# Hashed attention and a gated feed-forward layer on one core: row transfers on ACT's queue, preparation and weight steps at other places, another order of the products with v

## The chip, the cores and the metric

The kernel runs on one core of a Trainium2 chip. The metric is the device time of one execution in microseconds (us). Engines are named as in the profile: PE (matrix products; PEld is its weight load), DVE, ACT, POOL, and SP, which here only issues DMAs. Each engine works through its own instructions strictly in program order.

## The reference, cut to what matters

Four batches of eight heads, 768 positions, head dimension 64; then a feed-forward layer on 3072 rows of width 512 with hidden width 2048. A position attends only to positions with the same six hash bits.

```python
q_bits = (np.einsum('bhsd,dk->bhsk', q, proj) > 0)          # k_bits likewise, buckets from the bits
mask = q_bucket[:, :, :, None] == k_bucket[:, :, None, :]
scores = np.where(mask, scale * np.matmul(q, k.transpose(0, 1, 3, 2)), -1e9)
attn = np.exp(scores - scores.max(-1, keepdims=True))
attn = attn / (attn.sum(-1, keepdims=True) + 1e-09)
x = np.matmul(attn, v)                                       # heads side by side: 3072 x 512
h = x @ w_in
g = np.where(h >= 1, h, np.where(h <= -1, 0.0, (h + 1) ** 2 / 4.0))
out = g @ w_out
```

## The kernel before, in words

Every float32 operand is split into a high part and a low remainder, so that one exact product is several fp32r products. The 32 heads are worked in 16 **pairs**. A head has 12 **units** (two halves of the queries times six blocks of 128 keys), so a pair has 24. I call a unit's place in its pair its **phase**, 0 to 23; phases 0 to 11 are the even head, 12 to 23 the odd one. Units are numbered g = 0 to 383, and everything is emitted by one loop over g (written by hand; the schedule is not rearranged by anything later). For unit g the loop emits, in this order:

- `s_unit(g)`: two products on PE into one of four banks `s` (L439 and L440), then two exponentials on ACT, `ph` (L448, the high part) and the full value (L453), which goes to an SBUF tile `pf` if POOL is to subtract, and stays in the bank `s` if DVE is;
- `max_red` (L378): a row maximum on DVE over the tile `smax` that was filled at the end of the unit before, if there was one;
- `lo_unit(g-1)`: the low part `pl`, one subtraction (L39), on POOL for the key blocks that a table names, else on DVE;
- `pv_unit(g-4)`: three products with v on PE (L473, L475, L477) into one of two banks `o`. `PV_ORDER` gives the order in which a half's six blocks are taken. After the sixth, ACT copies the bank out (L483, `xs`);
- at every second unit two products `smax` (L361) for the maxima of a head that comes two heads later, at the end of phases 0, 2, 4 and so on. `smax` has one buffer, so these products wait until the reduction of the one before has read it;
- the tasks of unit g: preparation of later pairs and of the weights.

Tasks that the change touches, with the phase at which they stand before, for pairs from the third on:

- *Preparation of the pair after next* (`raw` to the operand tiles `t`): POOL does four quarters, a cast (L179) and a subtraction (L39), at phases 0, 2, 7, 11. SP issues moves between partitions (L190) at 13, 13, 14 and 18, and loads the next `raw` (L174) at 14.
- *Hash bits*: PE makes them at phases 5 and 17 (L237), ACT negates a part right there (`neg`, L243), DVE compares (L248) at 6 and 18, POOL scales at 19 (L307), SP writes four rows of bits (L316) at 20.
- *Row maxima*: at phases 5 and 17 `max_put` has ACT copy a small transposed tile `te` (L421); one DMA writes its first half as row 7 of an operand tile (`t<-te`, L423), another stores its second half (`em<-te`, L425). For heads 5 to 31, 27 of them, L423 is issued by SP; for heads 3 and 4 by ACT. The second product of a unit (L440) of that head needs row 7.
- *Weight conversion*: a block of weights is loaded as 8-byte numbers (`wraw`, SP, L78), ACT rebuilds the exponent (the scaled copy `wsq<-wraw`, L82), DVE does three steps on bits (L86, L90, L94; L86 writes in the bank `o` that `xs` was just copied from), POOL makes high and low parts (L102, L39), SP stores (`put`, L108). Twelve blocks of w_in start at phase 12 of an odd head with offsets 0, 9, 10, 11, 14, 19, 21, 23; twelve further blocks start at phase 0 of an even head with offsets 0, 9, 10, 11, 14, 16 (pairs 2 to 13). So in most pairs there are two scaled copies on ACT, at phases 9 and 21.
- `cast_v` (ACT, `va`, L323) stands at phase 6.

After unit 383 the feed-forward layer follows, from about 442 us on, which the change does not touch.

Of the kernel before, what the change touches and what calls it, by code (L numbers as in the profile page):

```python
# [11 lines left out]
F32 = mybir.dt.float32  # L12
# [29 lines left out]
def streamed(t):  # L42

    return t.rearrange("p (g r w) -> p g w r", r=2, w=4)


def into(t):
    return t.rearrange("p (g w r) -> p g w r", w=4, r=2)
# [71 lines left out]
NQK, NV, NP_ = 3, 2, 7  # L120
LAG = 4
POOL_J = (0, 3)
FROM = 4 * 12
QUARTER_J = ((0, 1, 3), (0, 3), (0, 1, 3), (0, 3))
PV_ORDER = (1, 2, 0, 4, 5, 3)
NU = 2 * NJ
SHIFT = 4


def attention(ctx, tc, wst, T1, T2, qk, v, pj, cv, x_d, s_d, e_d, tasks, shared):  # L130
    nc = tc.nc
# [286 lines left out]
    def max_put(hd):  # L418
        pr, h = hd // 2, hd % 2
        te = small.tile([2 * NJ, P], F32R, name="te")  # L420
        (nc.vector.tensor_copy if hd == 0 else nc.scalar.copy)(out=te, in_=mx.pop(hd)[0:2 * NJ, 0:P])  # L421
        if pr > 0:
            (nc.sync if hd > 4 else nc.scalar).dma_start(out=T2[pr % NQK][7:8, 0, h, :].bitcast(F32),  # L423
                                                         in_=te[0:NJ, :].bitcast(F32))
        nc.sync.dma_start(out=e_d[hd // H][hd % H:hd % H + 1, :], in_=te[NJ:2 * NJ, :].bitcast(F32))  # L425

# [2 lines left out]
    def pool_lo(g):  # L429
        return g % NJ in (QUARTER_J[g // NJ % 4] if FROM <= g < (NH - 2) * NU else POOL_J)  # L430

    def s_unit(g):
        hd, hf, j = g // NU, (g % NU) // NJ, g % NJ
        pr, h = hd // 2, hd % 2
        t1, t2 = T1[pr % NQK], T2[pr % NQK]
        sl = slice(hf * HS, (hf + 1) * HS)
        ks = slice(j * P, (j + 1) * P)
        ps = ps_s.tile([P, 512], F32, name="s")
        nc.tensor.matmul(out=into(ps[:, 0:HS]), lhsT=t1[:, 1, h, ks], rhs=streamed(t1[:, 0, h, sl]), start=True, stop=False)  # L439
        nc.tensor.matmul(out=into(ps[:, 0:HS]), lhsT=t2[:, 1, h, ks], rhs=streamed(t2[:, 0, h, sl]), start=False, stop=True)  # L440
        ph, pl = PH[g % NP_], PL[g % NP_]
        if hd >= NH - 2 and j == 4:
            pf = ps[:, 0:HS]
            nc.scalar.activation(out=pf, in_=pf, func=AF.Exp, scale=SCALE)
            nc.vector.tensor_copy(out=ph[:, 0:HS], in_=pf)
            units[g] = (pf, ph, pl)
            return
        nc.scalar.activation(out=ph[:, 0:HS], in_=ps[:, 0:HS], func=AF.Exp, scale=SCALE)  # L448
        if pool_lo(g):
            pf = work.tile([P, HS], F32, name="pf", bufs=3)  # L450
        else:
            pf = ps[:, 0:HS]
        nc.scalar.activation(out=pf, in_=ps[:, 0:HS], func=AF.Exp, scale=SCALE)  # L453
        units[g] = (pf, ph, pl)
# [7 lines left out]

    def pv_unit(n, between):
        hd, hf, jj = n // NU, (n % NU) // NJ, n % NJ
        j = PV_ORDER[jj]
        pr, h = hd // 2, hd % 2
        va, vb = VA[pr % NV], VB[pr % NV]
        _, ph, pl = units.pop(n - jj + j)
        o = obank[hf]
        w = HS if hf == 0 else HS + 8  # L470
        wa = va[:, j, h:h + 2, :].rearrange("p g d -> p (g d)")
        wb = vb[:, j, h:h + 2, :].rearrange("p g d -> p (g d)")
        nc.tensor.matmul(out=into(o[:, 0:w]), lhsT=wa, rhs=streamed(ph[:, 0:w]), start=(jj == 0), stop=False)  # L473
        between(3)
        nc.tensor.matmul(out=into(o[:, 0:w]), lhsT=wb, rhs=streamed(ph[:, 0:w]), start=False, stop=False)  # L475
        between(4)
        nc.tensor.matmul(out=into(o[:, 0:HS]), lhsT=wa, rhs=streamed(pl), start=False, stop=(jj == NJ - 1))  # L477
        if jj == NJ - 1:
            if hf == 0:
                xss[hd] = work.tile([P, S + 2], F32, name="xs")  # L480
            xs = xss[hd]
            w = HS if hf == 0 else HS + 2
            nc.scalar.copy(out=xs[:, hf * HS:hf * HS + w], in_=o[:, 0:w])  # L483
            if hf == 1:
                xss.pop(hd)
                rs, sr = 64 * h, 64 * (1 - h)
                nc.sync.dma_start(out=x_d[hd // H][rs:rs + 64, pr % (H // 2), :], in_=xs[rs:rs + 64])
                nc.sync.dma_start(out=s_d[hd // H][hd % H:hd % H + 1, :], in_=xs[sr:sr + 1, 0:S])
# [31 lines left out]
    def raw0():  # L520
        return wst.tile([P, DM, 2], I32, name="wraw").rearrange("p a b -> p (a b)").bitcast(F32)[:, 0:S].rearrange(
            "p (h s) -> p h s", h=1)
# [8 lines left out]
    def at(g, fn, *a):  # L531
        tasks[g].append((fn, a))

    first = [raw0(), raw0()]
# [106 lines left out]
    at(24, half_put, 2, 1)  # L641
    for h, g in enumerate((20, 2 * NU + 1)):
        at(g, lambda h=h: nc.gpsimd.memset(T2[0][32:33, 0, h].bitcast(F32), 0.0))
    for hd in range(NH):
        pr, h = hd // 2, hd % 2
        g = hd * NU
        if 0 < hd < NH - 2:
            gc, gt = ((30, 32), (41, 43))[hd - 1] if hd < 3 else (g + NU + SHIFT - 1, g + NU + SHIFT + 1)
            at(gc, max_clamp, hd + 2, nc.gpsimd)
            at(gt, max_tr, hd + 2)  # L650
            at(gt, max_put, hd + 2)
        if h == 0 and pr + 2 < NPAIR:
            g0 = g + (13, 2)[pr] if pr < 2 else g
            for n in range(4):
                gq = g0 + (n + (pr == 1 and n == 3) if pr < 2 else (0, 2, 7, 11)[n])
                at(gq, cast_h, pr + 2, nc.gpsimd, n % 2, n // 2)
                at(gq, low_h, pr + 2, nc.gpsimd, n % 2, n // 2)
            for n in range(2):
                at(g0 + (3 + (pr == 1) if pr < 2 else 13), move, pr + 2, n)
            at(g0 + (6 if pr < 2 else 14), move, pr + 2, 2)  # L660
            if pr + 3 < NPAIR:
                at(g0 + (7 if pr < 2 else 14), load_raw, pr + 3)
            bits_at = (((20, 1), (22, 0)), ((8, 1), (11, 0)))[pr] if pr < 2 else ((5, 1), (17, 1))
            for hf, (n, bank) in enumerate(bits_at):
                at(g + n, bits_mm, pr + 2, hf, bank)
                at(g + n + 1, bits_cmp, pr + 2, hf)
            at(g + n + 1, move, pr + 2, 3)
            if pr:
                at(g + n + 2, bits_scale, pr + 2, nc.gpsimd)
            else:  # L670
                at(g + 22, bits_scale, 2, nc.scalar, 0)
                at(g + 24, bits_scale, 2, nc.scalar, 1)
            at(g + (24, 18)[pr] if pr < 2 else g + 20, bits_put, pr + 2)
        if h == 0 and pr + 1 < NPAIR:
            gv = g + LAG + (2 if pr else 16)
            at(gv, cast_v, pr + 1, nc.scalar)
            for h, n in enumerate((1, 3) if pr < 2 else (12, 14)):
                at(gv + n, split_v, pr + 1, nc.gpsimd, h)
            if pr + 2 < NPAIR:
                at(gv + ((4, 6)[pr] if pr < 2 else 16), load_v, pr + 2)  # L680
# [7 lines left out]
    for i in range(2 * NJ):  # L688
        n = 5 * 31 + 35 * i // 4
# [500 lines left out]
def lsh_attn_ffn(ctx: ExitStack, tc: tile.TileContext, qk, v, pj, cv, w_in, w_out, out):  # L1190
    nc = tc.nc
# [8 lines left out]
    T2 = [wp.tile([P, 2, 2, S], F32R, name=f"t2_{i}") for i in range(NQK)]  # L1200
# [33 lines left out]
    def at(g, fn, *a):  # L1234
        tasks[g].append((fn, a))

    def conv(g, steps, offs):
        for fn, n in zip(steps, offs):
            at(g + n, fn)
# [6 lines left out]
    def wi_steps(i, cp, stage=None):  # L1246
        return ws.steps(win_v[:, :, i * P:(i + 1) * P, :], (P, NCT, P, 2), wih[i], wil[i], cp, stage, None, wq[i], word)
# [6 lines left out]
    for i in range(NW1):  # L1254
        if i < 2:
            conv((2 * i + 3) * NU, wi_steps(i, nc.scalar), (0, 9, 10, 11, 14 - (i == 0), 17, 19, 21))
        else:
            conv((2 * i + 3) * NU, wi_steps(i, nc.gpsimd), (0, 9, 10, 11, 14, 19, 21, 23))
    g0 = (NH - 4) * NU
    late = {}  # L1260
    for n in range(NSTG):
        i = n - (NFT - NW1)
        stage = wq[NW1 + n] if i < 0 else xdp.tile([P, DM], F32, name=f"wd{n}")
        if i < 0:
            first, late[n] = wi_steps(NW1 + n, nc.gpsimd, stage)
        elif i < 2:
            first, late[n] = wo_steps(i, nc.gpsimd, stage)
        else:
            first, late[n] = wo_steps(i, nc.scalar, stage, nc.gpsimd if i < 4 else nc.vector)
        conv((4 + 2 * n) * NU, first, (0, 9, 10, 11, 14, 16))  # L1270
    for n, g in enumerate((1, 7, 13, 25, 30, 35)):
        conv(g0 + g, late[n], (0, 5, 6))

# [1 line left out]
    for b in range(B - 1):  # L1275
        g = (b + 1) * H * NU + LAG + 4
# [32 lines left out]
    for i in range(2, NFT):  # L1309
        n = i + NFT - NW1  # L1310
# [71 lines left out]
```

## Time and profile before

| what | value |
|---|---|
| median of three runs | 928.15 us (926.03 to 929.7) |
| the profiled execution | 927.39 us, span 925.6 us |
| granted PE clock | full speed throughout |
| PE busy | 904.9 us, 98% of the span |
| DVE, ACT, POOL busy | 746.3, 667.1, 352.3 us |

The profiled execution's own time is 1.8 us over its span and 0.8 us under the median. The attention part is the first 442 us. There PE, DVE and ACT are all nearly full, POOL is busy for 350 us of it, and PE's queue is in program order; what delays PE there delays the end.

### The profile page before, as it was taken

Reading aid. Unit: us, or ns where it says so; the run is one execution under the profiler, and the core shown is the slowest. Engines: PE = TensorE matmul, PEld = TensorE weight load, DVE = VectorE, ACT = ScalarE, POOL = GpSimd, SP = SyncE. Lnnn points to the kernel's source line nnn. Section 1 sums busy time; section 2 is a strip of 40 time slices with the busy share of each in tenths; the row PEclk is TensorE's granted clock in tenths of the full one; section 3 lists DMA queues with packets and bytes.
Section 4 is the critical chain, followed back from the end, with each engine's and each line's share of the span. In section 5 each row is a group of like instructions: output and inputs, shape, how many; then the busy total and the mean of one; then the engine's idle time right before and its main releaser. Section 6 shows DMA issues by size and latency. Waiting matters only on the chain.

```text
span 925.6 us, 15771 instructions
## 1 busy us (share of the span) xinstructions
PE 904.9 (98%) x5050; PEld 846.4 (91%) x5050; DVE 746.3 (81%) x1319; ACT 667.1 (72%) x1471; POOL 352.3 (38%) x464
## 2 busy tenths in 40 slices
PE   8999999999999999999999999999999999999997
PEld 7789999999998999999999998989999999999996
DVE  8988889888897889887798888878877788765564
ACT  7889998999988999999656566555565555554454
POOL 7877777888787787778100000000000000000000
PEclk9999999999999999999999999999999999999999
DMA  5774676666666676564496388987559564464431
GB/s 159 195 201 109 181 195 194 191 181 180 175 179 187 188 193 184 140 185 123 144 307 228 114 245 299 317 259 204 149 152 271 156 200 127 147 178 126 125 91 68
DMA packets 95689, 167.66 MB, mean 181 GB/s; under 512 B 14532, under 2 KB 52536, under 8 KB 95608
## 3 DMA queue, kind: packets, MB, share of 16 engines
q1 hardware_dynamic: 95344, 166.63, 62.3%
q8 instruction: 40, 0.66, 0.3%
q14 instruction: 41, 0.34, 0.1%
q10 hardware_dynamic: 264, 0.03, 0.0%
HBM read 106.13 MB, written 33.96 MB: 151 GB/s over the span
## 4 chain that ended last, share of the span: by engine, by line
PE 71%; DVE 11%; ACT 7%; DMA 5%; issue 4%; POOL 1%; DVEq 0%; ACTq 0%; SPq 0%; POOLq 0%
PE y L913 24%; PE h L1145 16%; PE h L1050 6%; DMA t<-te 4%; PE s L440 4%; PE smax L361 4%; PE o L477 3%; PE o L473 3%; PE o L475 3%; PE s L439 3%; DVE nm L378 3%; DVE pl L39 3%; PE o L237 2%; ACT ph L448 2%; ACT s L453 1%
## 5 line engine op out<-in xcount | busy, mean ns | idle before, releaser
L448 ACT ACTIVATE ph<-s 128x384 fp32r<-128x384 f32 x380 | 193.0, 508 | 31.3 <-PE s L440 28.5
L39 POOL TENSOR_TENSOR pl<-pf,ph 128x384 fp32r<-128x384 f32 x154 | 156.0, 1019 | 67.9 <-ACT pf L453 67.7
L378 DVE TENSOR_REDUCE nm<-smax 128x1 f32<-128x768 f32 x168 | 160.1, 953 | 22.5 <-PE smax L361 19.4
L39 DVE TENSOR_TENSOR pl<-s,ph 128x384 fp32r<-128x384 f32 x230 | 123.6, 549 | 22.6 <-ACT s L453 18.3
L878 DVE SCALAR_TENSOR_TENSOR t<-t 128x384 f32<-128x384 f32 x128 | 71.3, 557 | 85.9 <-ACT z L873 85.6
L440 PE MATMUL s<-t 128*128 128x384 f32 x384 | 126.2, 329 | 3.5 <-DMA t<-te 3.4
L477 PE MATMUL o<-pl,va 128*128 128x384 f32 x384 | 125.7, 327 | 1.0 <-POOL pl L39 0.6
L473 PE MATMUL o<-ph,va 128*128 128x392 f32 (+1 forms) x384 | 126.0, 328 | 0.6 <-DVE neg L248 0.6
L475 PE MATMUL o<-ph,vb 128*128 128x392 f32 (+1 forms) x384 | 125.8, 328 | 0.0
L439 PE MATMUL s<-t 128*128 128x384 f32 x384 | 125.7, 327 | 0.0
L913 PE MATMUL y<-t,ghi 128*128 128x512 f32 x384 | 118.3, 379 | 0.7 <-DMA wc<-tmp 0.7
L453 ACT ACTIVATE s<-s 128x384 f32<-128x384 f32 x226 | 115.7, 512 | 0.0
L361 PE MATMUL smax<-t 128*128 128x384 f32 x336 | 85.9, 337 | 4.0 <-DVE nm L378 3.3
L883 ACT CAST ghi<-z 128x384 fp32r<-128x384 f32 x129 | 64.9, 503 | 32.0 <-DVE z L879 31.7
L873 ACT ACTIVATE z<-t,m 128x384 f32<-128x384 f32 x128 | 78.8, 615 | 4.2
L440 PEld LDWEIGHTS s<-t 128*128 128x128 f32 x384 | 72.5, 189 | 6.3 <-DMA t<-te 6.1
L913 PEld LDWEIGHTS y<-t,ghi 128*128 128x128 f32 x384 | 71.0, 189 | 7.4 <-ACT ghi L883 1.3
L453 ACT ACTIVATE pf<-s 128x384 f32<-128x384 f32 x154 | 77.5, 503 | 0.0
L1145 PE MATMUL h<-wbig,t 128*128 128x384 f32 x399 | 76.6, 326 | 0.3 <-DVE wsq L1164 0.3
L879 DVE TENSOR_TENSOR z<-t,z 128x384 f32<-128x384 f32 x128 | 71.4, 558 | 4.5
L477 PEld LDWEIGHTS o<-pl,va 128*128 128x128 f32 x384 | 72.6, 189 | 2.4 <-POOL pl L39 1.5
L913 PE MATMUL y<-woh,glo 128*128 128x512 f32 x192 | 73.1, 381 | 0.8 <-DVE glo L887 0.8
(208 smaller groups left out, 2003.3 us busy)
## 6 DMA issues: line engine op xcount, KB each, us to landing
t<-wc SPq DMA_DIRECT2D x92, 256.0 KB
t<-t SPq DMA_DIRECT2D x60, 384.0 KB
wraw<-wc SPq DMA_DIRECT2D x76, 256.0 KB
raw<-in_qk_dram SPq DMA_DIRECT2D x14, 768.0 KB
wraw<-in_w_in_dram SPq DMA_DIRECT2D x16, 512.0 KB
wraw<-in_w_out_dram SPq DMA_DIRECT2D x16, 512.0 KB
t<-ed SPq DMA_DIRECT2D x36, 192.0 KB
xd<-xs SPq DMA_DIRECT2D x32, 192.5 KB
```

The costliest lines, as they stand in the source:

```text
L39: eng.tensor_tensor(out=out, in0=a, in1=b, op=ALU.subtract)
L361: nc.tensor.matmul(out=into(ps[:, 0:HS]), lhsT=t2[:, 0, h, i * P:(i + 1) * P], rhs=streamed(t2[:, 1, h, hf * HS:(hf + 1) * HS]), start=Tru ...
L378: nc.vector.tensor_reduce(out=nmp(hd)[:, i:i + 1], in_=smax[hd][:, :, 0:HS], axis=AX.XY, op=ALU.max, negate=True)
L439: nc.tensor.matmul(out=into(ps[:, 0:HS]), lhsT=t1[:, 1, h, ks], rhs=streamed(t1[:, 0, h, sl]), start=True, stop=False)
L440: nc.tensor.matmul(out=into(ps[:, 0:HS]), lhsT=t2[:, 1, h, ks], rhs=streamed(t2[:, 0, h, sl]), start=False, stop=True)
L448: nc.scalar.activation(out=ph[:, 0:HS], in_=ps[:, 0:HS], func=AF.Exp, scale=SCALE)
L453: nc.scalar.activation(out=pf, in_=ps[:, 0:HS], func=AF.Exp, scale=SCALE)
L473: nc.tensor.matmul(out=into(o[:, 0:w]), lhsT=wa, rhs=streamed(ph[:, 0:w]), start=(jj == 0), stop=False)
L475: nc.tensor.matmul(out=into(o[:, 0:w]), lhsT=wb, rhs=streamed(ph[:, 0:w]), start=False, stop=False)
L477: nc.tensor.matmul(out=into(o[:, 0:HS]), lhsT=wa, rhs=streamed(pl), start=False, stop=(jj == NJ - 1))
L913: nc.tensor.matmul(out=into(ys[c][m]), lhsT=g_[:, m * P:(m + 1) * P], rhs=streamed(w), start=(first and k == 0), stop=(last and k == 2))
L1145: nc.tensor.matmul(out=into(ps), lhsT=w[:, cs], rhs=streamed(x), start=(n == 0 and s not in (2, 3, 6)), stop=(n == 5), skip_group_check=True)
```

## The change

The diff, with the lines that only bear new numbers left out:

```diff
-QUARTER_J = ((0, 1, 3), (0, 3), (0, 1, 3), (0, 3))
+QUARTER_J = ((0, 2, 3), (0, 3), (0, 2, 3), (0, 3))
 PV_ORDER = (1, 2, 0, 4, 5, 3)
+PV_LATER = (1, 0, 2, 4, 3, 5)
...
         if pr > 0:
-            (nc.sync if hd > 4 else nc.scalar).dma_start(out=T2[pr % NQK][7:8, 0, h, :].bitcast(F32),
+            nc.scalar.dma_start(out=T2[pr % NQK][7:8, 0, h, :].bitcast(F32),
...
-        j = PV_ORDER[jj]
+        j = (PV_LATER if n >= FROM else PV_ORDER)[jj]
...
-                gq = g0 + (n + (pr == 1 and n == 3) if pr < 2 else (0, 2, 7, 11)[n])
+                gq = g0 + (n + (pr == 1 and n == 3) if pr < 2 else (0, 2, 6, 9)[n])
...
-                at(g0 + (7 if pr < 2 else 14), load_raw, pr + 3)
+                at(g0 + (7 if pr < 2 else 13), load_raw, pr + 3)
...
-                at(g + n + 1, bits_cmp, pr + 2, hf)
+                at(g + n + (1 if pr < 2 else 2), bits_cmp, pr + 2, hf)
...
-                at(g + n + 2, bits_scale, pr + 2, nc.gpsimd)
+                at(g + n + (2 if pr < 2 else 3), bits_scale, pr + 2, nc.gpsimd)
...
-            at(g + (24, 18)[pr] if pr < 2 else g + 20, bits_put, pr + 2)
+            at(g + (24, 18)[pr] if pr < 2 else g + 21, bits_put, pr + 2)
...
-            conv((2 * i + 3) * NU, wi_steps(i, nc.gpsimd), (0, 9, 10, 11, 14, 19, 21, 23))
+            conv((2 * i + 3) * NU, wi_steps(i, nc.gpsimd), (0, 9, 10, 11, 14, 23, 25, 24))
...
-        conv((4 + 2 * n) * NU, first, (0, 9, 10, 11, 14, 16))
+        conv((4 + 2 * n) * NU, first, (0, 9, 10, 11, 14, 16) if n < 2 else (-6, 3, 10, 11, 14, 16))
```

Two places in the program, where the later argument stands. ACT, a pair in the middle (pair 8), phases 3 to 7, before; `xs` is the copy-out of the head before, `te` the small tile of row maxima, `neg` the negated part of the bits, `va` the cast of v:

```order
L483 COPY xs<-o_142 128x386
L448 ACTIVATE ph_159<-s 128x384
L453 ACTIVATE s<-s 128x384
L448 ACTIVATE ph_160<-s 128x384
L453 ACTIVATE s<-s 128x384
L421 CAST te<-s 12x128
L243 ACTIVATE neg<-o_142 32x384
L448 ACTIVATE ph_161<-s 128x384
L453 ACTIVATE pf<-s 128x384
L323 CAST va_156<-vraw 128x6x2x64
L448 ACTIVATE ph_162<-s 128x384
L453 ACTIVATE s<-s 128x384
```

The same place on ACT in the changed kernel:

```order
L484 COPY xs<-o_142 128x386
L82 ACTIVATE wsq<-wraw 128x512
L449 ACTIVATE ph_159<-s 128x384
L454 ACTIVATE s<-s 128x384
L449 ACTIVATE ph_160<-s 128x384
L454 ACTIVATE s<-s 128x384
L422 CAST te<-s 12x128
L424 DMA t_2_83<-te 1x6x128
L244 ACTIVATE neg<-o_142 32x384
L449 ACTIVATE ph_161<-s 128x384
L454 ACTIVATE pf<-s 128x384
L324 CAST va_156<-vraw 128x6x2x64
```

The scaled copy `wsq` has come ahead of phase 4 (before, it stands after the next `xs`, at phase 9), and the issue of the row transfer has come between `te` and `neg`. At phase 17 of every pair with bits the transfer's issue comes in the same way, with no scaled copy moved there.

DVE, phases 1 to 9 of a pair, before; `nm<-smax` is the row maximum, `wsq<-wsq,wsc,o` the last weight step, `pl` the low parts:

```order
L378 TENSOR_REDUCE nm<-smax 128x1
L94 SCALAR_TENSOR_TENSOR wsq<-wsq,wsc,o_141 128x512
L378 TENSOR_REDUCE nm<-smax 128x1
L39 TENSOR_TENSOR pl_171<-s,ph_164 128x384
L378 TENSOR_REDUCE nm<-smax 128x1
L39 TENSOR_TENSOR pl_166<-s,ph_159 128x384
L39 TENSOR_TENSOR pl_167<-s,ph_160 128x384
L248 TENSOR_TENSOR neg<-o_142,neg 32x384
L378 TENSOR_REDUCE nm<-smax 128x1
L39 TENSOR_TENSOR pl_169<-s,ph_162 128x384
L378 TENSOR_REDUCE nm<-smax 128x1
```

The same place on DVE in the changed kernel:

```order
L379 TENSOR_REDUCE nm<-smax 128x1
L39 TENSOR_TENSOR pl_170<-s,ph_163 128x384
L94 SCALAR_TENSOR_TENSOR wsq<-wsq,wsc,o_141 128x512
L379 TENSOR_REDUCE nm<-smax 128x1 x2
L39 TENSOR_TENSOR pl_166<-s,ph_159 128x384
L39 TENSOR_TENSOR pl_167<-s,ph_160 128x384
L379 TENSOR_REDUCE nm<-smax 128x1
L249 TENSOR_TENSOR neg<-o_142,neg 32x384
L39 TENSOR_TENSOR pl_169<-s,ph_162 128x384
L379 TENSOR_REDUCE nm<-smax 128x1
```

The low part of phase 1 has come to DVE, ahead of the weight step, and that of phase 2 has gone to POOL; the comparison `neg` stands behind the reduction of phase 7 instead of ahead of it. The low part `pl_169` (phase 7) still stands ahead of the reduction of phase 9.

## The prediction

> **What bounds the kernel now.** I read the page first, then a table by stretches, the list of waits, and the order of time of ACT, DVE and PE over one pair.
>
> ```profile
> span 925.6 us, 15771 instructions
> PE 904.9 (98%) x5050; PEld 846.4 (91%) x5050; DVE 746.3 (81%) x1319; ACT 667.1 (72%) x1471; POOL 352.3 (38%) x464
> ...
> 60.00:420.00 360.00, 351.82 (x2094) 336.99 (x2093) 313.16 (x470) 327.24 (x801) 281.57 (x355) 1.00 0.64 178
> 442.00:925.60 483.60, 476.70 (x2541) 442.18 (x2539) 365.16 (x711) 273.19 (x516) 2.50 (x2) 1.00 0.62 186
> ```
>
> The columns of the last two rows are the stretch, its length, and busy time of PE, PEld, DVE, ACT and POOL. From 60 to 420 us, where the change acts, PE is busy for 351.8 of 360 us, but ACT for 327.2 and DVE for 313.2: ACT has only 33 us to spare over 15 pairs, about 2 us a pair. What little PE loses is in the list of waits (total, times, longest):
>
> ```profile
> PEld smax L361 <- DVE nm L378: 11.7, 27, 0.6
> PEld s L440 <- DMA t<-te: 6.1, 9, 1.2
> PE s L440 <- DMA t<-te: 3.4, 6, 0.9
> PE smax L361 <- DVE nm L378: 3.3, 14, 0.3
> ```
>
> Two waits matter: for the row transfer, 3.4 (matrix engine idle) to 6.1 us (weight load idle), and for the row maximum on DVE, 3.3 to 11.7. So at most some 18 us can be won, by nobody's being late; but much more can be lost if ACT or DVE fall behind.
>
> **The row transfers.** SP issues 27 of them; two are already issued by ACT:
>
> ```profile
> L423 SPq DMA_DIRECT2D t<-te x27: 755/765/785, 81.8 to 425.3; - x27
> L423 ACTq DMA_DIRECT2D t<-te x2: 677/704/730, 57.7 to 70.5; - x2
> ...
> 57.45 0.25 ACT L421 CAST te<-s 12x128 fp32r<-12x128 f32 x1
> 57.73 0.73 ACTq L423 DMA_DIRECT2D t<-te  x1
> 58.51 0.48 ACT L243 ACTIVATE neg<-o 32x384 f32<-32x384 f32 x1 [0.81 <-PE o L477]
> ...
> PE o L473 <- DVE neg L248: 0.6, 1, 0.6
> ```
>
> An issue is not counted as busy, but it is not free: it starts after `te` has ended, lasts 0.73 us, and ACT's next instruction starts after it. From `te` to `neg` pass 1.06 us. The last row is that very place: ACT's `neg` came late, so DVE's comparison, so PE stood still for 0.6 us. On SP the same 0.77 us costs nothing, since SP computes nothing. Twenty-seven issues are 27 x 0.7 = 19 us of ACT in all; what they cost must be followed through the queues.
>
> **The scaled copy and the transfer, phases 3 to 14.** Pair 8, ACT:
>
> ```profile
> 238.12 0.52 ACT L448 ACTIVATE ph<-s 128x384 fp32r<-128x384 f32 x1
> ...
> 239.70 0.25 ACT L421 CAST te<-s 12x128 fp32r<-12x128 f32 x1
> 240.20 0.48 ACT L243 ACTIVATE neg<-o 32x384 f32<-32x384 f32 x1 [0.25 <-PE o L237]
> ...
> 242.56 0.50 ACT L453 ACTIVATE s<-s 128x384 f32<-128x384 f32 x1
> ...
> 244.49 0.52 ACT L483 COPY xs<-o 128x384 f32<-128x384 f32 x1
> 244.85 0.73 ACT L82 ACTIVATE wsq<-wraw 128x512 f32<-128x512 f32 x1
> 245.42 0.54 ACT L448 ACTIVATE ph<-s 128x384 fp32r<-128x384 f32 x1
> ```
>
> From 238.12 on ACT runs without a gap except the 0.25 ahead of `neg`. The scaled copy takes 245.42 - 244.85 = 0.57 of ACT's time. Moved ahead of 238.12, it shifts `te` to 240.27; with an issue behind it `neg` starts 1.06 later, at 241.33 in place of 240.20. The idle 0.25 is used up, and everything on ACT from there is 1.13 late, among it the exponential of phase 7 (242.56). At phase 9 the copy is no longer there, so from 245.42 on ACT is 0.56 late. What waits for phase 7 is DVE:
>
> ```profile
> 243.16 0.56 DVE L39 TENSOR_TENSOR pl<-s,ph 128x384 fp32r<-128x384 f32 x1 [0.86 <-ACT s L453]
> 243.63 0.95 DVE L378 TENSOR_REDUCE nm<-smax 128x1 f32<-128x768 f32 x1
> 244.50 0.55 DVE L39 TENSOR_TENSOR pl<-s,ph 128x384 fp32r<-128x384 f32 x1
> 245.04 0.69 DVE L86 TENSOR_SCALAR o<-wraw 128x512 int32<-128x512 int32 x1
> 245.64 0.95 DVE L378 TENSOR_REDUCE nm<-smax 128x1 f32<-128x768 f32 x1
> 246.51 0.55 DVE L39 TENSOR_TENSOR pl<-s,ph 128x384 fp32r<-128x384 f32 x1
> 246.97 0.75 DVE L90 SCALAR_TENSOR_TENSOR o<-wsq,wsc,o 128x512 int32<-128x512 int32 x1
> 247.63 0.55 DVE L39 TENSOR_TENSOR pl<-s,ph 128x384 fp32r<-128x384 f32 x1
> 248.10 0.95 DVE L378 TENSOR_REDUCE nm<-smax 128x1 f32<-128x768 f32 x1
> ...
> 244.72 0.51 PE L361 MATMUL smax<-t 128*128 128x384 f32 x2
> 246.70 0.54 PE L361 MATMUL smax<-t 128*128 128x384 f32 x2
> 249.10 0.59 PE L361 MATMUL smax<-t 128*128 128x384 f32 x2 [0.22 <-DVE nm L378]
> ```
>
> The low part at 243.16 waited 0.86 us for ACT; from there DVE works back to back to the reduction at 248.10, and PE's products `smax` must each wait for the reduction ahead of them. The first has 0.14 of room (244.72 against 243.63 + 0.95), the last has none and already waits. In the changed kernel this run of nine instructions has the same order, so it starts 1.13 late. The reduction of phase 9 then ends at 245.71, `smax` follows 0.05 behind it (as 249.10 does behind 248.10 + 0.95), at 245.76: PE is 1.04 late, and nearly 0.1 more because two `smax` behind a wait take 0.59 in place of 0.51. The waits at phases 12 and 14 keep their size, since the whole run has moved. PE's work from there is in order and has no gap in which to make it up. Price: 1.1 us in each of pairs 4 to 13, where both edits act: **+11**. Its ends: 0 if ACT made up its lateness somewhere that the rows don't show, and 10 x 1.34 (0.57 + 0.77, nothing absorbed) = +13.4. I take 11 because each step is a row. In pairs 2 and 3 the scaled copy stays at phase 9, and the issue alone makes 1.06 - 0.50 = 0.56 each: **+1** (0 to 1.5).
>
> **The transfer's other half, phases 17 to 2.**
>
> ```profile
> 226.94 0.48 ACT L243 ACTIVATE neg<-o 32x384 f32<-32x384 f32 x1 [0.19 <-PE o L237]
> ...
> 230.36 0.49 ACT L448 ACTIVATE ph<-s 128x384 fp32r<-128x384 f32 x1 [0.20 <-PE s L440]
> ...
> 234.69 0.95 DVE L378 TENSOR_REDUCE nm<-smax 128x1 f32<-128x768 f32 x1
> ...
> 228.07 5.25 DMA t<-te
> ...
> 233.37 0.43 PE L440 MATMUL s<-t 128*128 128x384 f32 x1 [0.44 <-DMA t<-te]
> 236.10 0.49 PE L361 MATMUL smax<-t 128*128 128x384 f32 x2
> ...
> 262.66 0.59 PE L361 MATMUL smax<-t 128*128 128x384 f32 x2
> ```
>
> On SP the transfer was issued at 228.07 and landed 5.25 us later; PE waited for it at 233.37. On ACT it is issued more than a microsecond sooner and stands behind no load, so I take this wait as gone. What is late next is the reduction at 234.69, done at 235.64: without the wait PE would reach `smax` at about 235.6 in place of 236.10, and must then wait for that reduction. ACT is late here too: the idle 0.19 and 0.20 absorb 0.4 of some 0.8, so the run of DVE up to 234.69 comes 0.2 to 0.4 later. With 0.3 that `smax` stands at 236.0 and the pair wins 0.1; pair 9, which had no wait for the transfer but already one of this kind (262.66, two products in 0.59), loses 0.3. Nine pairs of the first kind and three of the second: **0**, with ends at -6.1 (the whole wait won, nothing late next) and +4.8 (12 x 0.4).
>
> The Trainium skill ("DMA: Bandwidth & Descriptors", section "Rules for kernel authors") speaks against this edit: transfers from SP, ACT and GpSimd share the same 16 DMA engines, and spreading them only saves a sequencer's issue time. By that rule the wait would stay, and the sum would be some 3 us higher, the rival below; the same page's section "Queues, rings and completion order" has each engine take turns between queues packet by packet, which favours the small transfer. No row of this trace gives a landing on ACT's queue.
>
> **The rest.** The low part of phase 1 now stands on DVE ahead of the last weight step and costs 0.47 (243.16 to 243.63), so the reduction of phase 3 comes some 0.4 later. Its `smax` had about that much room, so at most 0.05 a pair: **+0.6** (0 to 3). The comparison behind the reduction of phase 7 or 19 takes 0.5 from in front of it; it then lies in the 0.86 that DVE waits anyway. It and the order 1 0 2 4 3 5, which gives POOL's block of phase 2 one more unit, can only win waits of a few tenths: **-1** (-3 to 0). POOL's quarters and weight steps, the earlier `raw` and the later rows of bits cost nothing as long as POOL's idle time (78 us of these 360) and SP's queue cover them; if that cover went, the rows of bits would be late for the next pair's `smax`, at phase 4. I price that at 0 (0 to +3).
>
> Sum: 11 + 1 + 0 + 0.6 - 1 = +11.6. The profiled execution took 927.39 us, 0.76 under the median: **939 us**.
>
> **Rivals.**
>
> *The added ACT time is hidden (faster).* For it: ACT has 33 us to spare, the wait for the transfer is 3.4 to 6.1, and a scaled copy leaves the place just ahead of the wait at 249.10. If DVE's run were held by the exponentials behind that copy, moving it would win up to 0.42 (249.10 against 246.70 and the step of 1.98 before it) in ten pairs, 4.2 us, and with 4.8 for the transfer, the middle of its two figures, 927.4 - 9.0 = 918. It decides whether phase 7's exponential comes later than the 0.1 of room that `smax` has at 244.72. Against: DVE does not wait for ACT anywhere after 243.16, and the spare time of ACT lies elsewhere.
>
> *The issue is cheaper on ACT than the two rows say.* At half its length the lateness is 0.57 + 0.39 - 0.25 = 0.7, 0.66 of it on PE; ten pairs 6.6, with 0.3 for two: 934.
>
> *The gains cancel it.* Transfer -4.8, DVE's order -3 (its end above), and half of the loss of 12: 927.4 - 1.8 = 926, or up to 930 if less is won.
>
> *The wait for the transfer stays*, because the 16 engines are as full as before (0.64 busy): then phases 0 to 2 cost some 3 us more: 942.
>
> **How the numbers follow.** About 0.5%, 4.6 us, is what a measurement tells from no change. My forecast 0.58 (935 to 944); cheaper issue 0.12; wait stays 0.07; cancelled 0.12; hidden 0.09; something worse, such as late rows of bits, 0.02. Slower: 0.58 + 0.07 + 0.12 + 0.02 = 0.79; same 0.12; faster 0.09. The range 926 to 945 leaves out the hidden case, the worst, and what lies under the cancelled one.
>
> **What would show it.** If I am right: 29 issues on ACT of 0.7 us, each followed by its next instruction; the wait of L440 for `te` gone; the wait of `smax` for `nm` grown from 11.7 (PEld) to over 20, much of it at phase 10; the stretch up to 442 us longer, the rest unchanged. I am wrong if DVE's wait for ACT at phase 7 is not about 1.1 longer, or if ACT's issues are much shorter.

## The result, and the profile after

| | median | range | to the kernel before |
|---|---|---|---|
| before | 927.50 us | 926.03 to 929.70 | |
| changed | 938.05 us | 937.36 to 939.18 | 1.0114 [1.0099, 1.0129] |

The changed kernel is 10.55 us slower; forecast were 939.0 us and 926 to 945. Medians and ratios in this document leave out two executions, one of the kernel before and one of `b_copy3`, that took more than 1160 us at a lower granted clock. The profiled execution took 938.72 us over a span of 936.9. First the page: span, busy time by engine, and the shares of the chain that ended last (before: PE 71%, DVE 11%, ACT 7%, DMA 5%).

```profile
span 936.9 us, 15856 instructions
...
PE 909.5 (97%) x5050; PEld 845.1 (90%) x5050; DVE 740.4 (79%) x1319; ACT 664.2 (71%) x1471; POOL 352.4 (38%) x464
...
PE 63%; ACT 14%; DVE 9%; DMA 5%; POOL 3%; issue 3%; ACTq 1%; SPq 1%; DVEq 0%; POOLq 0%
```

ACT and DVE are busy for a little less time than before (667.1 and 746.3 us), yet the span is 11.3 longer, and ACT has twice its share of the chain. An issue isn't counted as busy: what ACT lost does not stand in its busy time at all. Where it stands are the waits of the matrix engine and the rows of the transfer (duration in ns: least, median, most):

```profile
PEld smax L362 <- DVE nm L379: 23.6, 41, 1.4
PEld o L478 <- DVE pl L39: 5.1, 13, 0.5
...
PEld s L441 <- DMA t<-te: 0.3, 1, 0.3
```

```profile
L424 ACTq DMA_DIRECT2D t<-te x29: 677/683/732, 57.4 to 433.9; - x29
```

The wait of `smax` for the row maximum has doubled (11.7 before), the wait of the product with `pl` for DVE's low part has grown from 0.7 us in one place, and the wait for the row transfer (`s` for `t<-te`, 6.1 us in nine places before) is down to 0.3 us, once. The same pair 8 as in the prediction, ACT first:

```profile
242.32 0.49 ACT L484 COPY xs<-o 128x386 f32<-128x386 f32 x1
242.69 0.69 ACT L82 ACTIVATE wsq<-wraw 128x512 f32<-128x512 f32 x1
243.25 0.50 ACT L449 ACTIVATE ph<-s 128x384 fp32r<-128x384 f32 x1
...
244.81 0.25 ACT L422 CAST te<-s 12x128 fp32r<-12x128 f32 x1
245.10 0.68 ACTq L424 DMA_DIRECT2D t<-te  x1
245.82 0.48 ACT L244 ACTIVATE neg<-o 32x384 f32<-32x384 f32 x1 [0.76 <-PE o L478]
...
248.19 0.50 ACT L454 ACTIVATE s<-s 128x384 f32<-128x384 f32 x1
```

The 0.76 ahead of `neg` is put down to PE, but it is the issue of 0.68 and the 0.08 around it. The exponential of phase 7 ends at 248.69. DVE from there, then PE:

```profile
248.78 0.56 DVE L39 TENSOR_TENSOR pl<-s,ph 128x384 fp32r<-128x384 f32 x1 [1.45 <-POOL t L180]
249.26 0.95 DVE L379 TENSOR_REDUCE nm<-smax 128x1 f32<-128x768 f32 x1
250.12 0.55 DVE L39 TENSOR_TENSOR pl<-s,ph 128x384 fp32r<-128x384 f32 x1
250.67 0.69 DVE L86 TENSOR_SCALAR o<-wraw 128x512 int32<-128x512 int32 x1
251.27 0.95 DVE L379 TENSOR_REDUCE nm<-smax 128x1 f32<-128x768 f32 x1
```

```profile
249.40 0.43 PE L478 MATMUL o<-pl,va 128*128 128x384 f32 x1
250.26 0.59 PE L362 MATMUL smax<-t 128*128 128x384 f32 x2 [0.43 <-DVE nm L379]
...
252.33 0.54 PE L362 MATMUL smax<-t 128*128 128x384 f32 x2
...
254.73 0.59 PE L362 MATMUL smax<-t 128*128 128x384 f32 x2 [0.22 <-DVE nm L379]
```

DVE waits 1.45 us, in fact for ACT: 248.78 follows the exponential's end at 248.69. It then runs back to back in the order of before. `smax` at 250.26 follows 0.05 behind the reduction's end (249.26 + 0.95). The last `smax` waits 0.22, exactly as before. This is the place that the prediction named.

The table sums up where PE stands still in pairs 2 to 14, by phase. It is worked out from the starts of PE's products: the time from one start to the next, less what a product takes when it waits for nothing.

| us | phases 0–3 | 4–9 | 10–11 | 12–15 | 16–23 | sum |
|---|---|---|---|---|---|---|
| before | 7.72 | 1.88 | 0.66 | 6.48 | 3.88 | 20.6 |
| changed | 5.77 | 1.24 | 13.72 | 6.49 | 3.40 | 30.6 |

The sums differ by 10.0. The last unit of attention starts at 448.4 in place of 438.2, 10.1 later (from the unrounded starts); what follows takes 488.6 in place of 487.4. That part was not touched, and over the profiled executions of the experiments it took 487.2 to 489.2; that 1.2 us is left unexplained.

### The profile page after: what moved, and what is told of

It is laid out like the page before. It is cut to its first block, busy times and chain, and to the rows that moved or that the text cites. A ratio compares the mean times of both kernels' runs of the same rounds, so it can differ in the third digit from the quotient of the medians.

```text
span 936.9 us, 15856 instructions
## 1 busy us (share of the span) xinstructions
PE 909.5 (97%) x5050; PEld 845.1 (90%) x5050; DVE 740.4 (79%) x1319; ACT 664.2 (71%) x1471; POOL 352.4 (38%) x464
## 4 chain that ended last, share of the span: by engine, by line
PE 63%; ACT 14%; DVE 9%; DMA 5%; POOL 3%; issue 3%; ACTq 1%; SPq 1%; DVEq 0%; POOLq 0%
PE y L914 22%; PE h L1146 15%; PE h L1051 5%; ACT ph L449 5%; PE smax L362 4%; PE s L441 3%; DVE nm L379 3%; PE s L440 3%; ACT s L454 3%; PE o L474 3%; PE o L476 3%; PE o L478 3%; POOL pl L39 2%; DMA wc<-wbig 1%; ACT xs L484 1%
## 5 line engine op out<-in xcount | busy, mean ns | idle before, releaser
L362 PE MATMUL smax<-t 128*128 128x384 f32 x336 | 87.9, 343 | 12.3 <-DVE nm L379 12.0
L362 PEld LDWEIGHTS smax<-t 128*128 128x128 f32 x336 | 54.2, 188 | 26.8 <-DVE nm L379 23.6
```

The costliest lines, as they stand in the source:

```text
L362: nc.tensor.matmul(out=into(ps[:, 0:HS]), lhsT=t2[:, 0, h, i * P:(i + 1) * P], rhs=streamed(t2[:, 1, h, hf * HS:(hf + 1) * HS]), start=Tru ...
```

## The experiments

Two theories. *Lateness*: ACT's issue and the scaled copy each make ACT late at phase 7, and this reaches PE at phase 10. *Rival*: the loss comes from elsewhere in the change (preparation, weight steps, order), or the issue costs nothing and the copy all. All kernels compute the whole reference. The kernel before ran beside each group with a median of 927.65, 927.93 and 927.56 us.

**Undoing the two parts.** Each undone alone, then both:

```diff
a_sp:     -nc.scalar.dma_start(out=T2...            # t<-te, L424
          +(nc.sync if hd > 4 else nc.scalar).dma_start(out=T2...
a_copy9:  -(0, 9, 10, 11, 14, 16) if n < 2 else (-6, 3, 10, 11, 14, 16)
          +(0, 9, 10, 11, 14, 16)
a_both:   both
```

> The changed kernel with the 27 row transfers back on SP's queue, all else as changed. Lateness theory (what ACT is late by at phase 7 is what PE loses at phase 10, less 0.1): only the scaled copy is left, 0.57 less the idle 0.25 ahead of neg, so about 0.3 a pair at phases 10 and 11 in place of 1.07; with pairs 2, 3 and 14 some 11 us less, and 2 us back for the wait for the row transfer at phases 0 to 3: 929.5 us (928 to 931). If the scaled copy were the cause, 936 or more. If the order of the products and of POOL's work were, 938.

> The changed kernel with the scaled copies and their loads back at phases 9 and 0, transfers still issued by ACT. Lateness theory: the issue alone, 1.06 less 0.50, so 0.55 a pair at phases 10 and 11 in place of 1.07 in ten pairs: 933 us (931.5 to 934.5). If the scaled copy were the cause, 928 or less. If the issue alone or the order of the products were, 938.

> The changed kernel with both undone: order of products, POOL's table and preparation, the comparison, raw, bits and late weight steps are what is left of the change. Lateness theory: no loss at phase 10, the 2.8 us won behind the comparison and at single waits for POOL stay, the wait for the row transfer is back: 925 us (923.5 to 927.5). If the rest of the change cost time, 930 or more.

| | median | to before | phases 10–11 |
|---|---|---|---|
| changed | 938.05 | 1.0114 [1.0099, 1.0129] | 13.72 |
| issue back on SP (a_sp) | 927.45 | 0.9995 [0.9981, 1.0008] | 3.97 |
| copy back at phase 9 (a_copy9) | 933.40 | 1.0065 [1.0042, 1.0088] | 9.24 |
| both (a_both) | 924.09 | 0.9956 [0.9943, 0.9970] | 0.79 |

In the kernel with both undone, the same place of pair 8, DVE and PE:

```profile
242.57 0.56 DVE L39 TENSOR_TENSOR pl<-s,ph 128x384 fp32r<-128x384 f32 x1 [0.41 <-POOL t L180]
243.04 0.95 DVE L379 TENSOR_REDUCE nm<-smax 128x1 f32<-128x768 f32 x1
```

```profile
244.12 0.51 PE L362 MATMUL smax<-t 128*128 128x384 f32 x2
246.11 0.53 PE L362 MATMUL smax<-t 128*128 128x384 f32 x2
248.50 0.59 PE L362 MATMUL smax<-t 128*128 128x384 f32 x2 [0.22 <-DVE nm L379]
```

DVE waits 0.41 in place of 1.45, and `smax` at 244.12 waits for nothing. Of the three expectations two held; a_sp is 2.05 us faster than expected, since the wait for the row transfer, taken as 2 us, did not come back with SP's queue (0.7 us of weight load, once). The four kernels have one order on DVE and PE, so their lateness can be read against each other. Mean start in pairs 4 to 13, in us from the pair's first product on PE:

| | ACT `neg` | ACT phase 7 | DVE `pl` | PE phase 11 |
|---|---|---|---|---|
| a_both | 7.38 | 9.75 | 10.34 | 12.25 |
| a_sp: copy alone | 7.68 | 10.04 | 10.63 | 12.54 |
| a_copy9: issue alone | 8.02 | 10.39 | 10.98 | 12.88 |
| changed: copy and issue | 8.43 | 10.80 | 11.39 | 13.29 |

Lateness is handed on whole from column to column: 0.30, 0.64 and 1.05 at `neg`, and 0.29, 0.63 and 1.04 at PE. That the whole loss comes from these two parts is shown: without them the kernel is faster than before. The issue is the larger one.

**One issue more on ACT.** The second half's transfer, too:

```diff
-nc.sync.dma_start(out=e_d[hd // H]...              # em<-te, L426
+(nc.sync if hd < 5 else nc.scalar).dma_start(out=e_d[hd // H]...
```

> The changed kernel with ACT issuing the second transfer of each row tile too (em<-te, heads 5 to 31), so two issues in a row on ACT. Lateness theory: some 0.46 more at phase 5, all of it on PE at phase 10 in 12 pairs, and 0.2 to 0.3 more at phase 2 from the issue at phase 17: 946 us (943 to 948). If an issue on ACT were mostly hidden, 938 to 940.

```profile
L426 ACTq DMA_DIRECT2D em<-te x27: 463/469/1204, 82.6 to 448.1; - x27
```

952.27 us, 1.0261 [1.0236, 1.0285], 14.2 over the changed kernel: 6 more than expected. At phases 10–11 the loss went from 1.07 to 1.59 a pair: a second issue of 0.47 costs 0.52, as expected. Missed was phases 16–23, from 3.40 to 8.97: at phase 22 of pairs 2 to 12 `smax` now waits 0.4 us for its reduction, where it waited for nothing in the changed kernel. So at phase 17 the first issue was still absorbed, the second no more.

**Each part alone on the kernel before**, and the preparation and the comparison alone:

```diff
b_act:    L423 for all heads from nc.scalar
b_copy3:  the scaled copies from pair 4 on at -6, 3
b_prep:   -(0, 2, 7, 11)  +(0, 2, 6, 9);  load_raw 14 -> 13;  w_in's last offsets 19, 21, 23 -> 23, 25, 24
b_cmp:    bits_cmp n + 1 -> n + 2;  bits_scale n + 2 -> n + 3;  bits_put 20 -> 21   (from pair 2 on)
```

> The kernel before with one edit: ACT issues the 27 row transfers. Lateness theory: 0.56 at phase 10 in 12 pairs (6.7), 1 to 1.7 in pair 14, less 2 for the wait for the transfer at phase 0: 933.5 us (932 to 935). If the issue is hidden and the wait for the transfer falls away: 922 to 925.

> The kernel before with one edit: the scaled copy of ten weight blocks at phase 3 and its load six units sooner. Lateness theory: 0.57 less the idle 0.25, less 0.1 of room and 0.1 for two products behind a wait: 0.3 in ten pairs, 930.5 us (929 to 932). If the copy at phase 9 is what makes the wait at phase 14 (0.54 a pair): 922 to 924.

> The kernel before with POOL's quarters at phases 6 and 9, raw one unit sooner and POOL's late weight steps four units later, as in the change, and nothing else; the row transfers stay on SP. If the wait of L440 for the row transfer hangs on when raw (768 KB) is issued, it is gone here, and raw is issued at phase 10 or 11 in place of 15: phases 0 to 3 fall from 7.7 to some 5.5 us, 925.5 us in all (924 to 927). If it hangs on the queue, the wait stays, 5 to 6 us of it, and the time 927 to 928.

> The kernel before with the comparison of the bits behind the reduction, and with it scaling and the rows of bits one unit later, nothing else. If the comparison is what delays the reductions of phases 17 and 19 in pairs 4, 8 and 12, phases 16 to 23 lose 2 us in place of 3.9: 925.7 us. If the order of products or POOL's table won that, 927.5. If the later rows of bits come too late, 929 or more.

| | median | to before | phases 0–3 | 4–9 | 10–11 | 16–23 |
|---|---|---|---|---|---|---|
| b_act | 935.44 | 1.0072 [1.0049, 1.0094] | 7.71 | 2.94 | 6.83 | 4.98 |
| b_copy3 | 931.41 | 1.0038 [1.0023, 1.0053] | 7.64 | 4.62 | 2.46 | 3.85 |
| b_prep | 926.05 | 0.9986 [0.9977, 0.9995] | 5.12 | 0.85 | 0.90 | 5.77 |
| b_cmp | 926.78 | 0.9990 [0.9982, 0.9999] | 7.99 | 0.82 | 0.84 | 2.96 |

The issue alone costs 7.5 us, 1.9 more than expected, since the wait for the transfer stayed. The copy alone costs 3.5. That lies in the range expected, but partly by luck: phases 10–11 lost 1.8 in place of 3, and about 2 us stand at phase 4 of pairs 4, 7 and 11, which the expectation did not have; in pairs 4 and 11 the list puts 1.2 us of PE's wait there on late rows of bits (`t<-bits`). b_prep came out as expected; b_cmp won 0.9 us at phases 16–23 in place of 1.9. The most instructive is b_act. With the transfer on ACT's queue and nothing else changed, PE still waits for it:

```profile
PEld smax L361 <- DVE nm L378: 20.6, 41, 1.4
PEld s L440 <- DMA t<-te: 5.2, 6, 1.7
```

In b_act, pairs 6 and 7: SP's issue of the next `raw` (start, us), the transfer in the chain of waits, PE's wait, and the stretches of DMA (last but one column: share of the 16 engines):

```profile
200.03 1.81 SPq L174 DMA_DIRECT2D raw<-in_qk_dram  x1
```

```profile
203.19 6.74 DMA t<-te
```

```profile
209.97 0.43 PE L440 MATMUL s<-t 128*128 128x384 f32 x1 [0.55 <-DMA t<-te]
```

```profile
200.00:203.20 3.20, 3.20 (x21) 3.13 (x20) 2.67 (x5) 2.94 (x8) 2.85 (x5) 1.00 1.00 234
203.20:209.90 6.70, 6.22 (x38) 5.88 (x37) 5.56 (x10) 5.96 (x15) 4.00 (x5) 1.00 0.93 253
```

The 3 KB transfer follows `raw` by 3 us, while the 16 engines are full, and lands after 6.74 us. In b_prep SP issues it, but `raw` stands nine microseconds ahead:

```profile
191.19 0.54 SPq L174 DMA_DIRECT2D raw<-in_qk_dram  x1
200.28 0.77 SPq L423 DMA_DIRECT2D t<-te  x1
```

```profile
200.30:204.00 3.70, 3.70 (x25) 3.70 (x24) 2.93 (x5) 3.24 (x8) 2.12 (x4) 1.00 0.35 127
```

The engines are 0.35 busy, and b_prep's list has no row for this wait. `raw` can be issued sooner since SP waits less for POOL's quarters, for which the moves ahead of `raw` wait:

```profile
SPq L190 <- POOL t L179: 10.2, 9, 2.0
```

Before, that row reads 58.7, 14, 5.5. So the wait went with the time at which `raw` is issued, not with the queue: PE's weight load waits for the transfer for 6.1 us before (SP, late `raw`) and 5.2 in b_act (ACT, late), for 0.7 in a_sp (SP, early) and 0.3 in the changed kernel (ACT, early). An earlier `raw` was not tried apart from POOL's new places. b_prep gained 1.5 us only, since it brings a wait of its own, which the changed kernel, with its order 1 0 2 4 3 5, has not to this extent (1.2 there):

```profile
PEld o L477 <- POOL pl L39: 4.9, 12, 0.6
```

**Towards a faster kernel**: `best1` undoes the copy and keeps ACT's issue at phase 17 alone, where I thought it brought something (odd heads, phase 5, back on SP); `best2` is best1 with `cast_v` at phase 14; `best3` has both parts undone and `cast_v` at phase 14; `best4` is best3 with the weight steps' intermediate in SBUF (`wa`) in place of the bank `o`, which frees the steps from the bank, so that they could stand at later phases.

```diff
best1:  -nc.scalar.dma_start(   +(nc.sync if hd > 4 and hd % 2 else nc.scalar).dma_start(   and a_copy9
best2:  best1 and  -at(gv, cast_v, ...)   +at(gv + (8 if pr > 1 else 0), cast_v, ...)
best3:  a_both and the same cast_v
best4:  best3, wa for o, offsets (0, 9, 10, 16, 18, 23, 25, 24) and (0, 9, 10, 16, 17, 18)
```

> The changed kernel with the scaled copy back at phase 9, and ACT issuing the row transfers of even heads only (phase 17), SP those of odd heads (phase 5). Lateness theory: nothing late at phase 7, so no loss at phase 10; the wait for the transfer stays away (2 us), and the 2.8 us of the comparison and POOL stay: 922.7 us (921 to 925). If an issue on ACT costs time wherever it stands, 928 to 930.

> best1 with the cast of v on ACT at phase 14 in place of 6 from pair 2 on. Lateness theory: ACT is 0.72 earlier at phase 7, so DVE's run starts 0.3 earlier (then it waits for smax of phase 8) and the wait at phase 14 (0.54) shrinks by that much in 12 pairs: 919 us (917 to 921). If the cast then makes ACT late at phase 17, 922 to 925.

> a_both (row transfers on SP, scaled copy at phase 9) with the cast of v on ACT at phase 14 from pair 2 on. From best2, where this took the last waits at phases 10 to 15 down from 7.3 to 5.6 us: 922.5 us (921 to 924).

> best3 with DVE's second and third weight steps where DVE stood idle (phases 16 and 17 for blocks that start at phase 0, phases 4 and 6 for those that start at phase 12), the intermediate in SBUF in place of a bank o. If the waits for smax at phases 2 and 14 (0.47 and 0.54 a pair) are made by these steps' place between two reductions, they go: 12 us in 12 pairs at most, 912 us (910 to 916). If DVE or ACT is simply full there, 920 or more.

| | median | to before | sum of PE's stand-still |
|---|---|---|---|
| best1 | 926.04 | 0.9980 [0.9969, 0.9991] | 18.0 |
| best2 | 924.35 | 0.9957 [0.9942, 0.9971] | 15.2 |
| best3 | 922.21 | 0.9939 [0.9925, 0.9952] | 15.4 |
| best4 | 930.33 | 1.0026 [1.0013, 1.0038] | 25.0 |

best1 missed by 3.3: ACT's issue at phase 17 buys nothing, since the wait is gone already, and it costs 0.7 in pair 14; about 1.2 us more stand behind the last unit, where no edit acts (488.6 in place of 487.4 in a_both). best2 missed by 5.4: with `cast_v` gone from phase 6 the wait at phase 14 fell by 0.07 a pair (6.48 to 5.61 in twelve), because what holds it is DVE's own run of reductions, low parts and weight steps, not ACT. best4, which moves the weight steps, bears this out: its phases 10–15 lose nothing. best3 came out as expected, 0.3 under, and beats both kernels, by 5.35 us against before.

best4 should have won, and lost 8 us against best3. The wait at phase 14 went, as expected (phases 12–15 lose nothing, 5.6 us in best3). But phases 0–3 lose 14.9 us in place of 5.7, and 16–23 lose 8.2 in place of 2.5, most of it in waits of `smax` for DVE's reduction. DVE's steps on bits became slower, but only beside POOL. Two pieces of its order of time, and the same step in best3 (the first row from `o`, the second from `wa` in the feed-forward part, where POOL is idle):

```profile
233.74 1.00 POOL L39 TENSOR_TENSOR vb<-vraw,va 128x384 fp32r<-128x384 f32 x1
...
234.41 2.04 DVE L86 TENSOR_SCALAR wa<-wraw 128x512 int32<-128x512 int32 x1
234.71 1.00 POOL L39 TENSOR_TENSOR pl<-pf,ph 128x384 fp32r<-128x384 f32 x1
235.67 0.49 POOL L180 CAST t<-raw 128x384 fp32r<-128x384 f32 x1
...
243.52 1.00 POOL L39 TENSOR_TENSOR t<-raw,t 128x384 fp32r<-128x384 f32 x1
243.72 1.35 DVE L94 SCALAR_TENSOR_TENSOR wsq<-wsq,wsc,wa 128x512 int32<-128x512 int32 x1
```

```profile
L94 DVE SCALAR_TENSOR_TENSOR wsq<-wsq,wsc,o x24: 736/741/744, 77.1 to 377.8; 128x512 int32<-128x512 int32 x24
...
L94 DVE SCALAR_TENSOR_TENSOR wsq<-wsq,wsc,wa x8: 744/746/748, 460.3 to 510.2; 128x512 int32<-128x512 int32 x8
```

## Why the prediction was right, point by point

- **Phases 3 to 14, pairs 4 to 13: +11.** Right in mechanism and size. Each link is measured: against a_both, `neg` is 1.05 late (worked out 1.13), phase 7's exponential 1.05, the low part 1.05, PE 1.04, and PE's loss at phases 10–11 is 1.07 with the longer `smax`: 10.7 us. The sentence that DVE's wait at phase 7 would be 1.1 longer was too large: it is 0.59 longer than before (1.45 for 0.86), because before's pair also began with PE's wait for the transfer, and DVE's work ahead came 0.24 later. Against a_both, with the same order, it is 1.04 longer. The 33 us that ACT had to spare lie in about 13.6 pairs of 26.5 us, not 15; no term of the sum goes by that.
- **Pairs 2 and 3: +1.** Mis-sized: at phases 10–11 they lost 0.78 each more than before, not 0.56. The 0.56 was taken from pair 8, where ACT had idle 0.25 ahead of `neg`. In pair 2 a step on the weights (L100) keeps it busy, and `neg` follows `te` at once; ACT before, and then in the changed kernel:

```profile
81.56 0.25 ACT L421 CAST te<-s 12x128 fp32r<-12x128 f32 x1
81.84 0.48 ACT L243 ACTIVATE neg<-o 32x384 f32<-32x384 f32 x1
```

```profile
81.33 0.25 ACT L422 CAST te<-s 12x128 fp32r<-12x128 f32 x1
81.60 0.71 ACTq L424 DMA_DIRECT2D t<-te  x1
82.36 0.48 ACT L244 ACTIVATE neg<-o 32x384 f32<-32x384 f32 x1 [0.79 <-PE smax L362]
```

  From `te` to `neg` pass 1.03 in place of 0.28: the issue goes through whole, 0.75. **Pair 14** was not priced at all: it lost 0.78 at phases 10–11, and 0.96 at phases 16–23, together 1.7 us.
- **The transfer's other half, phases 17 to 2: 0.** The wait went, as forecast (0.3 us is left), and what was late next was, as forecast, the reduction ahead of phase 2's `smax` (5.5 us over pairs 2 to 13 in place of 1.7). The net was -2.0, inside the ends. But the step that said why is wrong. "Stands behind no load, so I take this wait as gone" is refuted by b_act: issued by ACT, the transfer took 6.7 to 7.6 us to land at phase 17 of pairs 6, 9, 10 and 11, where the chain of waits shows it (4.8 to 5.7 on SP's queue before), and the waits for it stayed, 5.2 us of weight load and 3.5 us of PE. That this term came out right is luck. What took the wait away is `raw`, issued at phase 10 or 11 in place of mostly 15, an effect of the preparation that I had priced at nothing. The Trainium skill's rule ("DMA: Bandwidth & Descriptors", "Rules for kernel authors": spreading transfers over issuing engines doesn't help, only issue time is saved) was weighed and put aside; b_act agrees with it, and saved issue time on SP was worth nothing, since SP computes nothing. The packet-by-packet turns that the Trainium skill describes on the same page (section "Queues, rings and completion order") did not shield the small transfer here, with 6.74 us for 3 KB. The rival "the wait stays" had the right rule and missed the other edit.
- **Low part of phase 1: +0.6, comparison and order: -1.** Small, and better than that. The phases 4–9 gained 0.6, among it 1.0 in pair 10, where `nmr` and `pl` had waited for POOL. Phases 18 and 20 of pairs 4, 8 and 12 gained 1.8 (0.6 a pair, down to nothing); b_cmp alone brought 0.9 of it, at phase 20. With -2.0 above, a_both shows what all the other edits are worth: -3.6 us, of which b_prep has 1.5 and b_cmp 0.8; the order of the products was not tried alone.
- **Rivals.** *Hidden* and *gains cancel it* are refuted by PE's rows at phase 10; *issue cheaper* by 29 issues with a median of 0.683 us.

The sum came within a microsecond in part by luck, because errors cancelled: about 2 us too little for pairs 2, 3 and 14, some 3 too much for the other edits (forecast -0.4, measured -3.6 in a_both), and 1.2 of the span in a part that no edit touched.

## What to carry to other kernels

Count an instruction that issues a DMA as full time of the engine that issues it, though the profile doesn't call it busy: here 0.68 us on ACT cost PE 0.63 us in each of pairs 4 to 13, where ACT had idle 0.25 us just there, and 0.78 in pairs 2 and 3, where it had none. The same issue at phase 17 cost nothing in these pairs, until a second one stood behind it (a_em). Before moving a small transfer to another queue, look at which large load shares the 16 engines with it, and move that load. Where an engine runs back to back, price a shift by following it from queue to queue to the first reader without room, and ask again in the pairs at the ends, where the room is another.

## What the runs showed of the hardware that I had not expected

While POOL is idle, a step on bits (L94) with both operands in SBUF takes as long as one with an operand in PSUM (0.746 and 0.741 us, rows above). Beside POOL it took 1.03 to 1.54 us in best4. Each of its 24 steps L94 in attention began while POOL was at work, and each ended 0.55 us after a POOL instruction that was running when it began, or that followed that one at once; as at 243.72: POOL ends at 244.52, DVE at 245.07. L86, one operand, has, but for one, two lengths there, 0.40 to 0.42 and (11 times) 2.02 to 2.06. Each of the long ones began with 0.33 us of a POOL subtraction still to run and another queued behind it, and ended 0.29 us after the cast that followed both. Beside ten of the short ones POOL was the slower one: its subtraction, which began 0.09 to 0.16 us earlier by the trace (its spans on POOL are rough), took 1.38 to 1.45 us in place of 1.02. This fits what the Trainium skill ("SBUF — State Buffer", section "Who interferes with whom") says: DVE and GpSimd share a pair of ports, and the one that comes second is blocked until the first has finished. It does not say why the long L86 waited for three POOL instructions in a row and not for one. That it is this pair of ports was not tested apart from these rows; they show that one of the two waits for the other, and that it is DVE in all 24 of L94. DVE's busy time between 60 and 420 us rose from 311.0 in best3 to 338.0 in best4. The bank `o` as an operand, which looks like a nuisance since it ties the steps to `xs`, kept DVE clear of POOL: in best3 L94 took 736 to 744 ns in attention, with POOL at work for 0.50 to 0.74 us of each.
